# A gate's logits moved from two extra matmul columns to VectorE, in a fused attention and MLP kernel

## The chip, the cores and the metric

The kernel runs on one core of one Trainium2 chip. The metric is device microseconds of one execution; a kernel's time is the median of its runs. One execution is also profiled by the hardware, and its span, from the first to the last instruction of the program, is what the views of the profile show. The engines are TensorE (PE, its weight loads PEld), VectorE (DVE), ScalarE (ACT), GpSimd (POOL) and SyncE (SP), which here issues the DMAs.

## The reference

With S = 2048 tokens of D = 448 features, 16 heads of 28 and an MLP of F = 1792 features, all in float32:

```python
g = sigmoid((x * gate_w).sum(-1, keepdims=True))
a = A(x, wqkv, wo)          # q, k, v = x @ wqkv; each token attends to 8 keys, two tokens apart,
                            # itself the first; softmax; o = attn @ v; a = o @ wo
b = B(x, w1, b1, w2, b2)    # relu(x @ w1 + b1)**2 @ w2 + b2
return g * a + (1 - g) * b
```

The change concerns `(x * gate_w).sum(-1)`, one number for each token: the gate's logit.

## The kernel before

Every matrix product is made from two parts of each float32 number, a high part (the number rounded to the matmul's input type, made by ScalarE) and a low part (the rest, a subtraction by VectorE). A product is then three products: high x high, high x low, low x high. The tokens are cut into four chunks of 512, with features on the partitions: three slabs of 128 features and a last one of 64, which lies twice, in partitions 0 to 63 and 64 to 127. A chunk's raw features come by one load into a tile `raw` (two buffers, rotating, shared with the raw weights), and are split there.

Phase A makes q, k and v. A token tile is 128 tokens, and q, k or v of one tile is an accumulator in PSUM (`Acc`) of 448 columns; q's has 450, since the weight of the gate stands in two more columns behind q's (`ncols`, NQ = D + 2; two, one of them unused). ScalarE copies column 448 of q's accumulator into `zt` (L214) behind the copy of q itself (L206), one number for each token. The products run in pairs on the two halves of the array's rows (`side_by_side`, L187): a matmul of 64 rows for one accumulator on rows 0 to 63, and beside it one for another accumulator on rows 64 to 127. A "step" is one such pair. An accumulator has 21 matmuls of 64 rows: 9 on each half (three slabs, three products) and 3 with the last slab. When it has had all of one half it goes over to the other, and for that `turn` writes one element of its bank (a 1x1 memset by VectorE, L197; ScalarE, L195, in one place): the next matmul into the accumulator waits for that write, and the write waits for the last matmul before it. In chunk 0, q's slabs run on the full height (L258) as the data come, and q's last slab runs beside k's. In chunks 1 to 3, `qkv_two` does a block of two token tiles in 63 steps: 12 steps of q0 beside k1, 12 of q1 beside k0, 12 of v0 beside v1; and then, with the halves exchanged, 9 steps of each pair. The resets of (q0, k1), (q1, k0) and (v0, v1) are issued behind steps 24, 36 and 42 and needed at steps 36, 45 and 54. Chunk 0's v (42 steps) has them behind steps 15 and 24, needed at 24 and 33.

The order of the other work is set by a planner's clock: `advance` adds a price for each group of matmuls (203 ns for one pair of 448 columns), and issues what is due. `when(t, fn)` puts work at the clock time t, in ns; `at(dt, fn)` at dt from now. A chunk's splits are four pieces, 900 ns apart, at 19000 (chunk 1), 35000 (chunk 2) and 53500 (chunk 3); the next chunk's load is 4500 behind. So each engine has a fixed order of instructions, and an engine that waits holds up what stands behind it. Attention (GpSimd's multiplications, VectorE's sums) starts once chunks 0 and 1 are stored to DRAM, and goes on through phase B, where the MLP's products and those with `wo` run. There `gates` (L394 to L397) turns `zt` into the gate and one minus the gate.

SP issues all loads and stores, in the order of the program. q, k and v go to DRAM by L212, the raw x tiles come by L561, the splits of x go to DRAM by L140, and the MLP's biases come by L704 and L705. The pool `smp` has two buffers with the tag "lg", used in turn: `halo0` (zeros for the first tokens' keys), and then the attention's logits, a tile for each unit.

Of the kernel before, what the change touches and what calls it, by code (L numbers as in the profile page):

```python
# [7 lines left out]
F32 = mybir.dt.float32  # L8
F32R = mybir.dt.float32r
AF = mybir.ActivationFunctionType  # L10
ALU = mybir.AluOpType
AX = mybir.AxisListType

S, D, H, DH, W, F = 2048, 448, 16, 28, 8, 1792
P = 128
# [6 lines left out]
NF = F // P  # L22
CH = 512
NQ = D + 2
NP = 512


# [29 lines left out]
def gated_mix_kernel(ctx: ExitStack, tc: tile.TileContext, xT, wqkv, w1, w2, wo, b1, b2, out):  # L57
    nc = tc.nc

    def f32(ap):  # L60
        return ap.bitcast(F32)
# [4 lines left out]
    k_d = tc.dram_tile([2, G, SP + HALO, C], F32, name="k_d")  # L66
    v_d = tc.dram_tile([2, G, SP + HALO, C], F32, name="v_d")
    x_d = tc.dram_tile([3, 4, P, 2, CH], F32, name="x_d")
    f_d = tc.dram_tile([2, NS, P, D], F32, name="f_d")


# [20 lines left out]
    smp = ctx.enter_context(tc.tile_pool(name="smp", bufs=2))  # L92
# [4 lines left out]
    zt, gt, g1t = zg[:, 0:2], zg[:, 2:4], zg[:, 4:6]  # L97
# [14 lines left out]
    def split_full(raw, hi, lo, soon=now):  # L112
        nc.scalar.activation(hi, raw, AF.Copy)
        soon(lambda: nc.vector.tensor_sub(lo, raw, f32(hi)))

    def split_x78(raw, x7, x8, soon=now):

        split_full(raw, x7, x8, soon)
# [15 lines left out]
    def x_split(raw, x, k):  # L134

        split_full(raw[:, k], x.h[k], x.l[k])
# [14 lines left out]
    xcp = actx.enter_context(tc.tile_pool(name="phase_a_own", bufs=1, reuse_waits="tile"))  # L151
    wqh = ap.tile([P, 3, NP + 2 * D], F32R, name="wqh")
    wql = ap.tile([P, 3, NP + 2 * D], F32R, name="wql")

    w7h = ap.tile([P, NP + D], F32R, name="w7h")
    w7l = ap.tile([P, NP + D], F32R, name="w7l")
    ap.tile([P, 48], F32, name="pad_a")
# [3 lines left out]

    stage = {}

    def ncols(b):
        return NQ if b == 0 else D

    def block(b):

        o = (0, NP, NP + D)[b]
        return slice(o, o + ncols(b))  # L170

    class Acc:

# [26 lines left out]
    def qkv_evacuate(pt, c, tl, b):  # L200
        par, t = c // 2, (c % 2) * 4 + tl
        first = (b, t // 2) not in stage
        if first:
            stage[b, t // 2] = xap.tile([P, G, 2, C], F32, tag="stage", name=f"st{c}_{tl}_{b}", bufs=ST_BUFS)
        st = stage[b, t // 2]
        nc.scalar.activation(st[:, :, t % 2], pt[:, :D].rearrange("p (g c) -> p g c", g=G), AF.Copy)  # L206
        if not first:
            stage.pop((b, t // 2))
            t0 = t - t % 2
            dst, off = ((q_d, 0), (k_d, HALO), (v_d, HALO))[b]  # L210
            dd = dst[par, :, off:off + SP].rearrange("g (p s) c -> p g s c", s=NS)[:, :, t0:t0 + 2]
            nc.sync.dma_start(dd.rearrange("p g s c -> p g (s c)"), st.rearrange("p g s c -> p g (s c)"))  # L212
        if b == 0:
            nc.scalar.activation(zt[:, par, t:t + 1], pt[:, D:D + 1], AF.Copy)  # L214

    def full(x, acc, tl, b, ks=range(3)):
        sl, n = slice(tl * P, tl * P + P), block(b)
        r = []
        for k in ks:
            r += [(acc, x.h[k][:, sl], wqh[:, k, n]), (acc, x.h[k][:, sl], wql[:, k, n]),  # L220
                  (acc, x.l[k][:, sl], wqh[:, k, n])]
        return r

    def last(x, acc, tl, b):

        sl = slice(tl * P, tl * P + P)
        n = block(1) if b == 2 else slice(0, ncols(b))
        h, l = w7h[:, n], w7l[:, n]
        return [(acc, x.x7[:, sl], h), (acc, x.x7[:, sl], l), (acc, x.x8[:, sl], h)]

    def accs(c, b, tls, tags):
        return [Acc(t, f"qkv{c}_{tl}_{b}", ncols(b)) for t, tl in zip(tags, tls)]

    def run(c, todo, steps):

# [13 lines left out]
    def qkv_first(x):  # L249


        four = range(4)
        q = accs(0, 0, four, "bbbb")
        for k in range(3):
            for two in ((0, 1), (2, 3)):
                for j, prods in enumerate(zip(*(full(x, q[i], i, 0, (k,)) for i in two))):
                    for acc, a, w in prods:
                        nc.tensor.matmul(acc.pt[:, :NQ], a, w, start=k == j == 0, stop=False)  # L258
            advance(12 * MM448)
        for acc in q:  # L260
            acc.todo = 3
        k = accs(0, 1, four, "mmmm")
        t = [sum((last(x, a[i], i, b) for i in four), []) for b, a in ((0, q), (1, k))]
        f = [full(x, k[i], i, 1) for i in four]
        run(0, [t[0] + f[0] + f[1] + f[2] + f[3], t[1] + f[2] + f[3] + f[0] + f[1]],
            [(3, [(0, 0, q[0])], (k[0], k[0])),
             (12, [(0, i, q[i]) for i in (1, 2, 3)], (k[1], k[1])),
             (24, [], (k[0], k[2])), (33, [], (k[1], k[3])),
             (39, [(1, 0, k[0]), (1, 2, k[2])]), (48, [(1, 1, k[1]), (1, 3, k[3])])])
        v = accs(0, 2, four, "bbbb")  # L270
        f, l = [full(x, v[i], i, 2) for i in four], [last(x, v[i], i, 2) for i in four]
        run(0, [f[0] + l[0] + f[2] + l[2] + f[1] + f[3], f[1] + l[1] + f[3] + l[3] + f[0] + f[2]],
            [(15, [], (v[0], v[1])), (24, [], (v[2], v[3])),
             (33, [(2, 0, v[0]), (2, 1, v[1])]), (42, [(2, 2, v[2]), (2, 3, v[3])])])
# [196 lines left out]
    def soon(fn):  # L471
        at(LO_DELAY, fn)

    def advance(dt):
        clock["pe"] += dt
        while due := [x for x in later if x[0] <= clock["pe"]]:
            item = min(due, key=lambda x: x[0])
            later.remove(item)
            item[1]()
        if not clock["on"]:  # L480
            clock["att"] = clock["pe"]
            return
        while clock["att"] < clock["pe"]:
            try:
                r = next(att)
            except StopIteration:
                clock["on"] = False
                return
            if r is None:
                clock["att"] = clock["pe"]  # L490
                return
            clock["att"] += r


    def raw_tile(name):
        return rawp.tile([P, 4, 512], F32, tag="raw", name=name)
# [62 lines left out]
    def x_load(c):  # L559
        raw = raw_tile(f"xraw{c}")  # L560
        nc.sync.dma_start(raw[:, :, :CH], xT[c])  # L561
        return raw
# [68 lines left out]
    raws = [raw_tile("wqraw0")]  # L631
    rx = raw_tile("xraw0")
    for k in range(4):
        if k < 3:
            nc.sync.dma_start(raws[0][:, k, :NQ], wqkv[0, :, k])  # L635
        else:
            for b, rows in ((0, slice(0, 64)), (1, slice(64, P))):
                nc.sync.dma_start(raws[0][rows, k, :NQ], wqkv[b, rows, k])
        for cols in ((slice(0, 256), slice(256, CH)) if k == 0 else (slice(0, CH),)):
            nc.sync.dma_start(rx[:, k, cols], xT[0, :, k, cols])  # L640

    for b, tag in ((1, "k"), (2, "v")):
        raw = attp.tile([P, 3, D], F32, tag=tag, name=f"wqraw{b}")
# [4 lines left out]
    nc.sync.dma_start(raw7, wqkv[2, :, 3, :D])  # L648
    x = x_tiles(0, xap)
    for k in range(3):  # L650
        nc.scalar.activation(wqh[:, k, :NQ], raws[0][:, k, :NQ], AF.Copy)
        halves = (slice(0, 256), slice(256, CH))
        for i, cols in enumerate(halves):

            if k == i == 0:
                nc.vector.tensor_copy(x.h[k][:, cols], rx[:, k, cols])
            else:
                nc.scalar.activation(x.h[k][:, cols], rx[:, k, cols], AF.Copy)  # L658
        nc.vector.tensor_sub(wql[:, k, :NQ], raws[0][:, k, :NQ], f32(wqh[:, k, :NQ]))
        for cols in halves:  # L660
            nc.vector.tensor_sub(x.l[k][:, cols], rx[:, k, cols], f32(x.h[k][:, cols]))
    split_full(raws[0][:, 3, :NQ], w7h[:, :NQ], w7l[:, :NQ])
    split_x78(rx[:, 3], x.x7, x.x8)

    def wq_split(b, k):
        if k < 3:
            split_full(raws[b][:, k], wqh[:, k, block(b)], wql[:, k, block(b)])
        else:
            split_full(raw7, w7h[:, NP:], w7l[:, NP:])

    def when(t, fn, *args):
        later.append((t, lambda: fn(*args)))

    xs, xm = {0: x}, {}
    xraw = {1: x_load(1)}
# [30 lines left out]
        wq_split(1, k)  # L708
    for k in range(4):
        when(12000.0 + k * 900.0, wq_split, 2, k)  # L710
    for c, t in SPLIT_AT.items():
        when(t, x_begin, c)
        for k in range(4):
            when(t + k * 900.0, lambda c, k: x_split(xraw[c], xs[c], k), c, k)
        if c < 3:
            when(t + 4500.0, x_more, c + 1)
            when(t + 5000.0, lambda c: x_spill(c, xs[c]), c)
# [321 lines left out]
    c, x = ORDER[0], xm[3]  # L1039
# [8 lines left out]
    for g in range(2, 2 * NF):  # L1048
        i, f = g // (NF // 2), g % (NF // 2) * 2
        c = ORDER[i]  # L1050
# [118 lines left out]
```

## Time and profile before

| | us |
|---|---|
| median of 3 runs | 414.45 (414.34 to 414.81) |
| span of the profiled execution | 412.7 |
| TensorE busy in it | 408.2 |
| VectorE busy | 255.7 |
| ScalarE busy | 211.3 |
| GpSimd busy | 268.5 |

The page gives the profiled execution's span; of the time around it, it says nothing. A line of the timeline has: start in us from the span's start, duration in us, engine, line of the kernel, operation, names of out and in, shapes, and how many instructions of the same kind were merged, with the idle time before them and what ended it. A line of a group has, behind the bar, the busy time in us, the mean of one instruction in ns, and the idle time before. Matmuls are pipelined, so the duration of one (0.36 us) is longer than the distance from one to the next on the same rows; the distance is what counts. A line of windows has the stretch, its length, TensorE's busy time with the count of matmuls (a few records are missing), the granted clock, and the DMA's share and GB/s.

### The profile page before, as it was taken

The numbers are of one execution on the slowest core, as the hardware profiler recorded it, in microseconds if no ns is written. First come the engines' busy times: TensorE is split into PE (matmuls) and PEld (weight loads), VectorE is DVE, ScalarE is ACT, GpSimd is POOL, SyncE is SP. The second block draws the span as 40 slices with busy tenths as digits, with TensorE's granted clock in tenths as the row PEclk, the third lists the DMA queues.
The fourth block names the chain that finished last, engine by engine and source line by source line (L and its number), as shares of the span: only waits on it lengthen the run. The fifth ranks groups of instructions, "written<-read, shape, count | busy, mean of one in ns | idle before, by whom it ended". The sixth has DMA issues, their size and how long they took to land.

```text
span 412.7 us, 9327 instructions
## 1 busy us (share of the span) xinstructions
PE 408.2 (99%) x3835; PEld 378.0 (92%) x3835; DVE 255.7 (62%) x404; ACT 211.3 (51%) x477; POOL 268.5 (65%) x167
## 2 busy tenths in 40 slices
PE   8999999999999999999999999999999999999997
PEld 7999999999999999888888888989898888888996
DVE  4520433276767766777656798879576677891354
ACT  4641656388765565444565535444653254346540
POOL 0000001955999999989989899999899977940000
DMA  7989999969362315555112649764146630168304
GB/s 226 380 324 326 268 393 299 335 213 311 101 235 104 128 42 218 209 184 152 29 58 95 228 160 270 197 146 149 27 163 186 229 129 2 45 177 132 96 0 180
DMA packets 65611, 73.76 MB, mean 179 GB/s; under 512 B 32352, under 2 KB 58528, under 8 KB 65184
## 3 DMA queue, kind: packets, MB, share of 16 engines
q1 hardware_dynamic: 65568, 73.16, 55.1%
q8 instruction: 30, 0.49, 0.5%
q14 instruction: 13, 0.11, 0.1%
HBM read 45.71 MB, written 28.25 MB: 179 GB/s over the span
## 4 chain that ended last, share of the span: by engine, by line
PE 97%; DMA 1%; SPq 0%; DVE 0%; ACT 0%; issue 0%
PE b L187 33%; PE h L187 32%; PE qkv L187 23%; PE a L187 7%; PE qkv L258 1%; DMA xraw<-xT 1%; PE a L943 1%; PE last L943 0%; SPq L640 0%; SPq L635 0%; DVE bt L822 0%; ACT x L658 0%; PE last L935 0%; PE a L935 0%
## 5 line engine op out<-in xcount | busy, mean ns | idle before, releaser
L334 POOL TENSOR_TENSOR qk<-q,k 128x896 f32<-128x896 f32 x64 | 135.1, 2137 | 84.8 <-DMA k<-k_d 76.4
L341 POOL TENSOR_TENSOR av<-lg,v 128x896 f32<-128x896 f32 x64 | 119.4, 1961 | 6.3 <-DVE lg L335 5.8
L187 PE MATMUL qkv<-wqh,x 64*128 64x448 f32 (+1 forms) x528 | 89.1, 361 | 0.0
L615 DVE TENSOR_TENSOR h<-h,h 128x512 fp32r<-128x512 f32 x56 | 38.4, 688 | 65.9 <-ACT h L618 65.5
L187 PEld LDWEIGHTS qkv<-wqh,x 64*128 64x128 f32 x528 | 72.2, 184 | 0.8
L187 PE MATMUL qkv<-wql,x 64*128 64x448 f32 (+1 forms) x264 | 72.2, 360 | 0.0
L187 PE MATMUL b<-w2ah,h 64*128 64x448 f32 x448 | 68.5, 359 | 0.0
L187 PE MATMUL b<-w2bh,h 64*128 64x448 f32 x448 | 67.8, 360 | 0.0
L335 DVE TENSOR_REDUCE lg<-qk 128x32 f32<-128x896 f32 x64 | 67.0, 1074 | 0.0
L349 DVE TENSOR_REDUCE o<-av 128x112 f32<-128x896 f32 x64 | 66.4, 1070 | 0.1
L616 ACT ACTIVATE h<-h,b1z 128x512 f32<-128x512 f32 x56 | 36.7, 655 | 43.6 <-PE h L187 43.6
L187 PEld LDWEIGHTS b<-w2ah,h 64*128 64x128 f32 x448 | 46.9, 184 | 2.8
L187 PEld LDWEIGHTS b<-w2bh,h 64*128 64x128 f32 x448 | 45.3, 184 | 3.2 <-ACT h L567 0.3
L187 PEld LDWEIGHTS qkv<-wql,x 64*128 64x128 f32 x264 | 44.5, 184 | 0.4
L187 PE MATMUL b<-w2al,h 64*128 64x448 f32 x224 | 44.3, 358 | 0.0
L187 PE MATMUL b<-w2bl,h 64*128 64x448 f32 x224 | 43.2, 358 | 0.0
L206 ACT ACTIVATE st<-qkv 128x448 f32<-128x448 f32 x48 | 24.3, 546 | 34.8 <-PE qkv L187 26.9
L617 ACT ACTIVATE h<-h 128x512 fp32r<-128x512 f32 x56 | 33.5, 598 | 1.7
L618 ACT ACTIVATE h<-h 128x512 f32<-128x512 f32 x56 | 33.3, 594 | 0.0
L187 PE MATMUL h<-x,w1h 64*128 64x512 f32 x168 | 32.8, 386 | 0.0
L567 ACT ACTIVATE h<-h 128x4 fp32r<-128x4 f32 (+1 forms) x35 | 7.2, 207 | 43.1 <-PE b L187 43.0
L187 PE MATMUL h<-x2b,w1h 64*128 64x512 f32 x168 | 28.2, 386 | 0.0
(145 smaller groups left out, 728.7 us busy)
## 6 DMA issues: line engine op xcount, KB each, us to landing
k<-k_d SPq DMA_DIRECT2D x8, 840.0 KB, 6.4
v<-v_d SPq DMA_DIRECT2D x8, 840.0 KB, 4.8
x_d<-x SPq DMA_DIRECT2D x11, 512.0 KB, 6.6
q_d<-st SPq DMA_DIRECT2D x8, 448.0 KB, 4.1
k_d<-st SPq DMA_DIRECT2D x8, 448.0 KB, 4.6
v_d<-st SPq DMA_DIRECT2D x8, 448.0 KB, 5.9
w1raw<-w SPq DMA_DIRECT2D x4, 896.0 KB, 9.2
q<-q_d SPq DMA_DIRECT2D x8, 448.0 KB, 3.6
```

The source lines that it names most:

```text
L187: nc.tensor.matmul(acc.pt[:, :acc.n], a[rows], w[rows], start=acc.todo == acc.all, stop=acc.todo == 1)
L206: nc.scalar.activation(st[:, :, t % 2], pt[:, :D].rearrange("p (g c) -> p g c", g=G), AF.Copy)
L258: nc.tensor.matmul(acc.pt[:, :NQ], a, w, start=k == j == 0, stop=False)
L334: nc.gpsimd.tensor_mul(pr, q[:, s:s + 1].to_broadcast([P, W, C]), k[:, s:s + W])
L335: pending.append(lambda: nc.vector.tensor_reduce(lg[:, s], pr.rearrange("p w (h d) -> p w h d", h=HG), axis=AX.X, op=ALU.add))
L341: nc.gpsimd.tensor_mul(pr.rearrange("p (h d) w -> p w h d", h=HG), lg[:, s][:, :, :, None].to_broadcast([P, W, HG, DH]), v[:, s:s + W].rea ...
L349: nc.vector.tensor_reduce(o[:, g * C:(g + 1) * C], pr, axis=AX.X, op=ALU.add)
L567: nc.scalar.activation(ap, f32(ap), AF.Copy)
L615: nc.vector.tensor_sub(hl, pt, f32(hh))
L616: ops += [lambda pt=pt, r=r: nc.scalar.activation(pt, pt, AF.Relu, bias=b1t[:, f + r:f + r + 1]), lambda pt=pt, hh=hh: nc.scalar.activatio ...
L617: lambda pt=pt, hh=hh: nc.scalar.activation(hh, pt, AF.Square),
L618: lambda pt=pt, r=r, low=low: (nc.scalar.activation(pt, pt, AF.Square), at(delays[r], low))]
```

## The change

q's accumulators get 448 columns; `ncols` goes, and so does the copy of column 448 (L214). The logits are made by VectorE from the raw features: for each chunk, `z_product` multiplies slab 0 by its weight (one number for each partition, `gw`) and adds slabs 1, 2 and the last (64 partitions) by fused multiply-adds into a tile `zu` of 128x512. `z_sums` transposes `zu` in blocks of 32x32 and sums each block's 32 numbers: for each token four partial sums remain, in four blocks of partitions. After the last chunk these are stored to DRAM (32 KB) and loaded back by four loads so that the four partial sums of a token stand in one partition, and `z_last` adds them into `zt`. The tile `zs` that holds them takes the second "lg" buffer, so the attention's tiles exchange buffers. The products stand between the splits of the same chunk, 450 ns behind each by the planner's clock.

```diff
-    def ncols(b):
-        return NQ if b == 0 else D
...
-        return slice(o, o + ncols(b))
+        return slice(o, o + D)
...
-        if b == 0:
-            nc.scalar.activation(zt[:, par, t:t + 1], pt[:, D:D + 1], AF.Copy)
...
-        return [Acc(t, f"qkv{c}_{tl}_{b}", ncols(b)) for t, tl in zip(tags, tls)]
+        return [Acc(t, f"qkv{c}_{tl}_{b}", D) for t, tl in zip(tags, tls)]
...
-                        nc.tensor.matmul(acc.pt[:, :NQ], a, w, start=k == j == 0, stop=False)
+                        nc.tensor.matmul(acc.pt[:, :D], a, w, start=k == j == 0, stop=False)
...
+    zs = smp.tile([P, 3, NZ], F32, tag="lg", name="zs")
+    zu = xcp.tile([P, CH], F32, tag="zu", name="zu")
+    zpart, zall, gw = zs[:, 0], zs[:, 1], zs[:, 2, 0:4]
+    nc.vector.tensor_copy(gw, raws[0][:, :, D])
+    def z_product(raw, k):
+        r = slice(0, P if k < 3 else 64)
+        if k:
+            nc.vector.scalar_tensor_tensor(zu[r], raw[r, k], gw[r, k:k + 1], zu[r], op0=ALU.mult, op1=ALU.add)
+        else:
+            nc.vector.tensor_scalar_mul(zu, raw[:, 0], gw[:, 0:1])
+    def z_sums(c):
+        nc.vector.transpose(zu, zu)
+        nc.vector.tensor_reduce(
+            zpart.rearrange("p (b c t) -> p c t b", b=4, c=4)[:, c],
+            zu.rearrange("p (t b r) -> p t b r", t=4, b=4), axis=AX.X, op=ALU.add)
+    def z_store():
+        nc.sync.dma_start(z_d, zpart)
+    def z_load():
+        for b in range(4):
+            nc.sync.dma_start(
+                zall[b * 32:b * 32 + 32].rearrange("p (a n) -> p a n", a=4),
+                z_d[:, b * 16:b * 16 + 16].rearrange("(a c) n -> c a n", a=4))
+    def z_last():
+        nc.vector.tensor_reduce(
+            zt.rearrange("p q s -> p (q s)"), zall.rearrange("p (a n) -> p n a", a=4), axis=AX.X, op=ALU.add)
...
+    for k in range(4):
+        when(15000.0 + k * 700.0, z_product, rx, k)
+    when(17900.0, z_sums, 0)
+    when(60500.0, z_store)
+    when(76000.0, z_load)
+    when(86500.0, z_last)
     for c, t in SPLIT_AT.items():
         when(t, x_begin, c)
         for k in range(4):
             when(t + k * 900.0, lambda c, k: x_split(xraw[c], xs[c], k), c, k)
+            when(t + k * 900.0 + 450.0, lambda c, k: z_product(xraw[c], k), c, k)
+        when(t + 4200.0, z_sums, c)
```

More of the change, by code (lines that the diff above doesn't have):

```diff
@@ L24 @@
 NQ = D + 2
+NZ = 64
 NP = 512
@@ L68, in gated_mix_kernel @@
     x_d = tc.dram_tile([3, 4, P, 2, CH], F32, name="x_d")
+    z_d = tc.dram_tile([P, NZ], F32, name="z_d")
     f_d = tc.dram_tile([2, NS, P, D], F32, name="f_d")
@@ L226, in last @@
         sl = slice(tl * P, tl * P + P)
-        n = block(1) if b == 2 else slice(0, ncols(b))
+        n = block(1) if b == 2 else slice(0, D)
         h, l = w7h[:, n], w7l[:, n]
@@ L650, in gated_mix_kernel @@
     for k in range(3):
-        nc.scalar.activation(wqh[:, k, :NQ], raws[0][:, k, :NQ], AF.Copy)
+        nc.scalar.activation(wqh[:, k, :D], raws[0][:, k, :D], AF.Copy)
         halves = (slice(0, 256), slice(256, CH))
@@ L658, in gated_mix_kernel @@
                 nc.scalar.activation(x.h[k][:, cols], rx[:, k, cols], AF.Copy)
-        nc.vector.tensor_sub(wql[:, k, :NQ], raws[0][:, k, :NQ], f32(wqh[:, k, :NQ]))
+        nc.vector.tensor_sub(wql[:, k, :D], raws[0][:, k, :D], f32(wqh[:, k, :D]))
         for cols in halves:
             nc.vector.tensor_sub(x.l[k][:, cols], rx[:, k, cols], f32(x.h[k][:, cols]))
-    split_full(raws[0][:, 3, :NQ], w7h[:, :NQ], w7l[:, :NQ])
+    split_full(raws[0][:, 3, :D], w7h[:, :D], w7l[:, :D])
     split_x78(rx[:, 3], x.x7, x.x8)
+    zs = smp.tile([P, 3, NZ], F32, tag="lg", name="zs")
[23 more added lines that the diff above has]
+            zt.rearrange("p q s -> p (q s)"), zall.rearrange("p (a n) -> p n a", a=4), axis=AX.X, op=ALU.add)
     def wq_split(b, k):
```

## The prediction

> **What bounds the kernel now.** I read the page first: engines' shares, then the waits of TensorE.
>
> ```profile
> span 412.7 us, 9327 instructions
> PE 408.2 (99%) x3835; PEld 378.0 (92%) x3835; DVE 255.7 (62%) x404; ACT 211.3 (51%) x477; POOL 268.5 (65%) x167
> PE 97%; DMA 1%; SPq 0%; DVE 0%; ACT 0%; issue 0%
> ```
>
> TensorE is busy for 99% of the span and makes 97% of the chain that ended last. Its list of waits has two entries, both before 9 us:
>
> ```profile
> PE warm L628 <- DVE b1z L626: 1.2, 1, 1.2
> PE qkv L258 <- ACT x L658: 0.3, 1, 0.3
> ```
>
> So time can be won only by fewer or faster matmuls, and lost only where some other engine makes TensorE wait where it does not now. The change takes two columns from q's products, 450 to 448. What a column costs is read from the timeline of TensorE, in a place where one row half runs q (450) and the other k (448):
>
> ```profile
> 35.03 0.36 PE L187 MATMUL qkv<-w7h,x 64*128 64x448 f32 x1
> 35.23 0.36 PE L187 MATMUL qkv<-w7l,x 64*128 64x448 f32 x1
> 35.24 0.55 PE L187 MATMUL qkv<-w7h,x 64*128 64x450 f32 x2
> 35.44 0.37 PE L187 MATMUL qkv<-w7l,x 64*128 64x450 f32 x1
> 35.65 0.37 PE L187 MATMUL qkv<-w7h,x 64*128 64x450 f32 x1
> 35.86 0.53 PE L187 MATMUL qkv<-wqh,x 64*128 64x448 f32 x2
> ```
>
> 448 columns step by 0.200 us (35.03 to 35.23). 450 columns step by 0.207 us (35.24, 35.44, 35.65, 35.86: 0.62 us in three steps). Two columns cost 6.7 ns, far more than 2/448 of 200 ns (0.9 ns). The same shows in whole blocks. These windows are cut at the first 450-column product of each block of 63 steps (two token tiles: q, k and v); the first window is chunk 0's v, 42 steps of 448 columns alone:
>
> ```profile
> 22.50:30.90 8.40, 8.40 (x87) 1.00 0.88 309
> 30.90:43.66 12.76, 12.76 (x130) 1.00 0.94 313
> 43.66:56.42 12.76, 12.76 (x129) 1.00 1.00 320
> 56.42:69.18 12.76, 12.76 (x129) 1.00 1.00 323
> 69.18:81.94 12.76, 12.76 (x128) 1.00 0.99 341
> 81.94:94.72 12.78, 12.78 (x127) 1.00 0.73 243
> ```
>
> 8.40/42 is 0.200 us a step. A block of 63 such steps would take 12.60 us and takes 12.76. The missing 0.16 us is exactly 24 steps of 6.7 ns: in a block's first part q0 and then q1 run 12 steps each on the same row half (9 full, 3 of the last 64 features). In the second part q has 9+9 steps on the other half, 0.12 us, which the lead of that half covers. The granted clock (1.00) is full throughout.
>
> **The change part by part.**
>
> Removed, q's two columns. Six blocks at 0.16 us are 0.96 us (the sixth, from 94.72, has MLP work beside it but the same 24 steps). In chunk 0, the 12 last-feature products of q run beside k's: 12 x 6.7 ns = 0.08 us. Chunk 0's 36 full-height products are 450 wide too, but step by 0.200 already:
>
> ```profile
> 9.82 0.96 PE L258 MATMUL qkv<-wqh,x 128*128 128x450 f32 x4
> ```
>
> (busy 0.96 us for four: three steps of 0.200 and the 0.36 us of the last), so I take 0 there; bounds 0 and 36 x 6.7 ns = 0.24. Sum: 1.04 us. The Trainium skill, "TensorE: Matmul & The Clock Gate", section Back-to-back issue gap, gives an isolated warm gap of N/2.4 + 2.5 ns, so an estimate of 0.8 ns for two columns; by it the sum would be 156 x 0.8 ns = 0.13 us and no measurable change. The trace disagrees (200 and 207 ns where the page gives 189 and 190), and the measurement decides.
>
> Removed, 16 copies of the logit column on ScalarE.
>
> ```profile
> L214 ACT ACTIVATE zg<-qkv x16: 142/166/191, 14.2 to 109.5; 128x1 f32<-128x1 f32 x16
> ```
>
> 16 x 0.17 us on an engine that is 51% busy and for which TensorE never waits: nothing.
>
> Added, VectorE work: for each of four chunks a scaling (128x512), three fused multiply-adds, a transposition and a sum over 32. Prices, by the nearest groups:
>
> ```profile
> L822 DVE SCALAR_TENSOR_TENSOR bt<-b,zg,bt 128x448 f32<-128x448 f32 x16 | 10.2, 680 | 7.9 <-PE b L187 7.8
> L114 DVE TENSOR_TENSOR x<-xraw,x 128x512 fp32r<-128x512 f32 x13 | 8.4, 690 | 14.1 <-ACT x L113 14.1
> L661 DVE TENSOR_TENSOR x<-xraw,x 128x256 fp32r<-128x256 f32 x6 | 2.4, 422 | 1.8 <-ACT x L658 1.8
> L656 DVE CAST x<-xraw 128x256 fp32r<-128x256 f32 x1 | 0.3, 294 | 2.6 <-DMA xraw<-xT 2.6
> L352 DVE STREAM_TRANSPOSE o<-o 128x448 f32<-128x448 f32 x16 | 10.2, 638 | 0.3
> L349 DVE TENSOR_REDUCE o<-av 128x112 f32<-128x896 f32 x64 | 66.4, 1070 | 0.1
> ```
>
> An element costs (690-422)/256 = 1.05 ns. Multiply-add at 512: 680+67 = 0.75 us, about 0.68 from start to start where the next does not depend on it. Scaling: one source, like the cast, 256 elements in 294 ns; at 512 between 0.43 (fixed part 155 ns, half the slope) and 0.69; I take 0.43, nearest the cast. Transposition 0.71, sum 1070-384x1.05 = 0.67. A chunk costs 4.1 us, all four 16 us on an engine 62% busy. What matters is what queues behind them: the resets of a PSUM accumulator (1x1 memsets, L197) that let its second row half go on. Chunk 1's splits, from the timeline of VectorE, and TensorE's step 24 of v:
>
> ```profile
> 19.21 0.62 DVE L114 TENSOR_TENSOR w7l<-wqraw,w7h 128x448 fp32r<-128x448 f32 x1
> 24.23 1.93 DVE L114 TENSOR_TENSOR x<-xraw,x 128x512 fp32r<-128x512 f32 x3 [4.40 <-ACT x L113]
> 25.52 0.06 DVE L197 MEMSET qkv<- 1x1 f32 x2
> 27.52 0.09 DVE L197 MEMSET qkv<- 1x1 f32 x2 [0.75 <-PE qkv L187]
> 27.23 0.43 PE L187 MATMUL qkv<-wqh,x 64*128 64x448 f32 x2
> ```
>
> Chunk 0's sums fit the gap from 19.83 to 24.23 (4.1 of 4.4 us). Then in the new order: split 0.62, scaling 0.37, split 0.62, first resets (25.9, needed at 27.23), multiply-add, split, multiply-add, split (2.6): second resets done by 28.6. They are needed at step 33, 27.23 + 9 x 0.2 = 29.03. Some 0.35 us is left after the handover. For chunk 2 and chunk 3:
>
> ```profile
> 41.90 1.29 DVE L114 TENSOR_TENSOR x<-xraw,x 128x512 fp32r<-128x512 f32 x2 [3.19 <-ACT x L113]
> 46.81 0.06 DVE L197 MEMSET qkv<- 1x1 f32 x2
> 58.34 2.54 DVE L114 TENSOR_TENSOR x<-xraw,x 128x512 fp32r<-128x512 f32 x4 [5.84 <-ACT x L113]
> 61.60 0.14 DVE L197 MEMSET qkv<- 1x1 f32 x2 [0.72 <-PE qkv L187]
> ```
>
> Chunk 2: splits, products, sums (6.4 us from 41.90) and two w1 splits (1.2): reset at 49.5, needed at 43.66 + 36 x 0.2 = 50.86; 1.1 us left. Chunk 3: before the second reset stand 4 splits and 6 new instructions, 6.5 us from 58.34: 64.9, needed at 56.42 + 45 x 0.2 = 65.42; about 0.45 left. So I price the stalls at 0. Bounds: 0 from below (a longer VectorE queue shortens nothing), above with the scaling at 0.69 and the sum 0.4 dearer, 0.3 us in all.
>
> Moved, the buffers. The raw x tiles are held by the products too: the load of chunk 1 (issued at 11.31) also waits for the copy of the weight column, about 0.7 us later; chunk 3's (46.17) for chunk 2's last product, some 0.9 later.
>
> ```profile
> 11.31 0.33 SPq L561 DMA_DIRECT2D xraw<-xT  x1
> 46.17 0.50 SPq L561 DMA_DIRECT2D xraw<-xT  x1
> DMA to landing us min/median/max: 2.5/5.6/7.9
> ```
>
> With the longest landing of such a load, 7.9 us, they are there by 19.9 and 55.0; the splits that use them reach VectorE at 24.23 and 58.34. The two "lg" buffers trade places, which orders nothing new in time. Nothing.
>
> Added, DMAs on SP: one store of 32 KB and four loads of 64-byte runs, due at clock 60.5 and 76.0 of the planner, that is near 65 and 82 us. Ahead of v's store:
>
> ```profile
> 74.44 1.11 SPq L704 DMA_DIRECT2D b1z<-b  x1
> 83.20 0.67 SPq L212 DMA_DIRECT2D v_d<-st  x1
> ```
>
> b1's load has runs of 56 bytes and takes 1.11 us to issue; four such are 4.4 at most, so v_d of chunk 2 goes up to 3 us later. Only unit 4 of the attention reads it, much later. The last sum (0.2 us) comes behind the third reset of chunk 3's first block, near 92. The four loads are issued by 86 and land by 92 (median above) to 94 (longest). What VectorE would lose there it has idle before the next resets, near 100:
>
> ```profile
> 98.30 0.63 DVE L518 TENSOR_TENSOR w2al<-copy,w2ah 128x448 fp32r<-128x448 f32 x1 [1.71 <-ACT copy L513]
> ```
>
> I price it at 0, with a bound of 0.3 us (2 us late less 1.7 idle).
>
> Sum: -1.04 us on the profiled span, 412.7 to 411.7. The page gives no time of that execution outside its span; the median of the runs is 414.45, 1.75 more, and I let that stand: 413.4.
>
> **The rivals.**
> 1. The columns are not the cause of 0.207 (two unequal streams, or uneven issue, and the step stays). Every 12.76 against 12.60, with 24 steps to account for it, speaks against; that 450 columns at full height step by 0.200 speaks for. The Trainium skill's gap rule, named above, would lead here too. Time 414.3 to 414.45. Half the effect, or 0.3 to 0.5 us lost in resets (second bound above), ends in the same class: about 413.9.
> 2. The resets come late and TensorE stalls: slower. Let each added VectorE instruction cost e more than my price. The stalls are 3e-0.35 (chunk 1), 6e-1.1 (chunk 2), 6e-0.45 (chunk 3), together 15e-1.9. The gain is gone at e = 0.20 us, at 0.25 it is slower by 0.2%, at 0.30 the time is 414.45-1.04+2.6 = 416.0. The prices rest on measured groups of the same operations, which speaks against; that multiply-adds with both operands in SBUF appear in no row speaks for.
>
> **How the numbers follow.** 0.2% (0.83 us) is about what a measurement of this kernel can tell from no change. My sum of 1.04 is only a little above it. Main case, gain of 0.85 to 1.2: 0.55. Rival 1 with the partial cases: 0.30. Rival 2: 0.15. So faster 0.55, same 0.30, slower 0.15. The main case's own range is 413.1 to 413.6 (with 0.24 more at the full-height products, or 0.2 lost). For 8 in 10 it reaches through rival 1 and the beginning of rival 2: 413.0 to 414.9.
>
> **What would show it.** After: blocks of 12.60 us and steps of 0.200 in q; the same two waits of TensorE and none on L197; multiply-adds of 0.75 us; the second resets of chunk 1 near 0.4 us before step 33; span 411.7. The prediction is wrong if blocks stay at 12.76, if TensorE waits for a memset near 29, 51 or 65 us, or if a later engine gives the 1 us back.

## The result

The median went from 414.56 us (22 runs, 414.33 to 416.12) to 413.81 us (22 runs, 413.37 to 415.26). The ratio is 0.9978, with a 95% interval of 0.997 to 0.9987: 0.9 us by the ratio (0.5 to 1.2 by the interval), 0.75 by the medians, where 1.04 had been forecast. On another chip the same two kernels gave 0.9969 (0.9956 to 0.9983).

The page of the changed kernel (busy time, share of the span and instructions of each engine):

```profile
span 412.0 us, 9325 instructions
PE 407.2 (99%) x3835; PEld 371.7 (90%) x3835; DVE 270.5 (66%) x430; ACT 210.5 (51%) x461; POOL 268.5 (65%) x167
```

Its TensorE's waits: us in total, their count, and the longest in us:

```profile
PE warm L625 <- DVE b1z L623: 1.2, 1, 1.2
PE qkv L255 <- ACT x L655: 0.3, 1, 0.3
```

VectorE's share rose from 62% to 66%, by 15 us of work, and TensorE waits for the same two things as before. The gain is in the pace of phase A. These rows of TensorE's timeline are the first step with the last slab (the tenth step) of the six blocks of 63 steps:

```profile
32.58 0.36 PE L186 MATMUL qkv<-w7h,x 64*128 64x448 f32 x2
45.18 0.36 PE L186 MATMUL qkv<-w7h,x 64*128 64x448 f32 x2
57.78 0.36 PE L186 MATMUL qkv<-w7h,x 64*128 64x448 f32 x2
70.38 0.36 PE L186 MATMUL qkv<-w7h,x 64*128 64x448 f32 x2
82.98 0.37 PE L186 MATMUL qkv<-w7h,x 64*128 64x448 f32 x2
95.65 0.39 PE L186 MATMUL qkv<-w7h,x 64*128 64x448 f32 x2
```

The first five are 12.60 us apart, where the kernel before takes 12.76; the last distance is 12.67, where it takes 12.78. VectorE's new work, by groups (busy time, mean ns; the last slab's four multiply-adds, on 64 partitions, are a group of their own), and chunk 1's splits in its timeline:

```profile
L671 DVE SCALAR_TENSOR_TENSOR zu<-xraw,zs,zu 128x512 f32<-128x512 f32 x8 | 6.0, 746 | 0.1
L677 DVE STREAM_TRANSPOSE zu<-zu 128x512 f32<-128x512 f32 x4 | 2.8, 711 | 0.1
L678 DVE TENSOR_REDUCE zs<-zu 128x16 f32<-128x512 f32 x4 | 2.8, 688 | 0.1
L673 DVE TENSOR_SCALAR zu<-xraw,zs 128x512 f32<-128x512 f32 x4 | 1.9, 480 | 0.0
```

```profile
24.11 0.69 DVE L116 TENSOR_TENSOR x<-xraw,x 128x512 fp32r<-128x512 f32 x1 [0.18 <-ACT x L115]
24.72 0.48 DVE L673 TENSOR_SCALAR zu<-xraw,zs 128x512 f32<-128x512 f32 x1
25.80 0.06 DVE L196 MEMSET qkv<- 1x1 f32 x2
28.36 0.06 DVE L196 MEMSET qkv<- 1x1 f32 x2
```

Chunk 0's sums were done 0.18 us before chunk 1's first split, and the second resets were done at 28.4, some 0.5 us before step 33 needed them.

To see where the time came from, two places are compared that every version passes: the first step with the last slab in chunk 0, and ScalarE's first activation of the MLP, at the end of phase A. First the kernel before, then the changed one:

```profile
12.71 0.47 PE L187 MATMUL qkv<-w7h,x 64*128 64x450 f32 x2
111.25 0.66 ACT L616 ACTIVATE h<-h,b1z 128x512 f32<-128x512 f32 x1 [0.87 <-PE h L187]
```

```profile
12.67 0.48 PE L186 MATMUL qkv<-w7h,x 64*128 64x448 f32 x2
110.37 0.66 ACT L613 ACTIVATE h<-h,b1z 128x512 f32<-128x512 f32 x1 [0.94 <-PE h L186]
```

From the one place to the other the kernel before takes 98.54 us and the changed one 97.70: 0.84 us less. The start up to 12.7 us depends on when the first loads land (ScalarE's first splits wait for them), and among the profiled executions below it lies between 12.39 and 13.02 wherever nothing was changed in it. That is why single spans differ by a few tenths. Phase B changed little: VectorE's last instruction comes at 409.72 before and at 408.79 after, 0.93 earlier, and the span is 0.75 shorter (412.73 and 411.98), since from there to the end it took 3.01 us before and 3.19 after. The last store lies in that stretch.

### The profile page after: what moved, and what is told of

Its sections match the earlier page's. It is cut to its first block, busy times and chain, and to the rows that moved or that the text cites. A ratio compares the mean times of both kernels' runs of the same rounds, so it can differ in the third digit from the quotient of the medians.

```text
span 412.0 us, 9325 instructions
## 1 busy us (share of the span) xinstructions
PE 407.2 (99%) x3835; PEld 371.7 (90%) x3835; DVE 270.5 (66%) x430; ACT 210.5 (51%) x461; POOL 268.5 (65%) x167
## 4 chain that ended last, share of the span: by engine, by line
PE 97%; DMA 1%; SPq 0%; DVE 0%; ACT 0%; issue 0%
PE b L186 33%; PE h L186 32%; PE qkv L186 23%; PE a L186 7%; PE qkv L255 1%; DMA xraw<-xT 1%; PE a L984 1%; PE last L984 0%; SPq L637 0%; SPq L632 0%; DVE bt L863 0%; ACT x L655 0%; PE last L976 0%; PE a L976 0%
## 5 line engine op out<-in xcount | busy, mean ns | idle before, releaser
L186 PE MATMUL qkv<-wqh,x 64*128 64x448 f32 x528 | 78.6, 359 | 0.0
L186 PEld LDWEIGHTS qkv<-wqh,x 64*128 64x128 f32 x528 | 50.7, 184 | 2.7
L186 PE MATMUL qkv<-wql,x 64*128 64x448 f32 x264 | 48.8, 359 | 0.0
L186 PEld LDWEIGHTS b<-w2bh,h 64*128 64x128 f32 x448 | 42.8, 184 | 3.3 <-ACT h L564 0.3
L186 PEld LDWEIGHTS b<-w2ah,h 64*128 64x128 f32 x448 | 43.1, 184 | 2.9
L186 PE MATMUL b<-w2al,h 64*128 64x448 f32 x224 | 41.2, 358 | 0.0
L186 PE MATMUL b<-w2bl,h 64*128 64x448 f32 x224 | 41.1, 358 | 0.0
L186 PE MATMUL h<-x,w1h 64*128 64x512 f32 x168 | 29.6, 386 | 0.0
L186 PE MATMUL h<-x0b,w1h 64*128 64x512 f32 x168 | 28.1, 386 | 0.0
L186 PE MATMUL h<-x1b,w1h 64*128 64x512 f32 x168 | 28.1, 386 | 0.0
```

Source lines behind the costliest of these rows:

```text
L186: nc.tensor.matmul(acc.pt[:, :acc.n], a[rows], w[rows], start=acc.todo == acc.all, stop=acc.todo == 1)
```

## The experiments

**The removal alone.** The logits are left out: zeros stand in their place.

```diff
-    zs = smp.tile([P, 3, NZ], F32, tag="lg", name="zs")
...
-        when(t + 4200.0, z_sums, c)
+    nc.gpsimd.memset(zt, 0.0)
```

> The removal alone: q's accumulators have 448 columns and the gate's logits are left out (zeros instead, no work on VectorE, no DMAs for them). Theory: the whole gain comes from the two columns and VectorE's work is hidden, so the time is that of the changed kernel, 413.5 to 413.8 us, span 411.6 to 412.0, and TensorE at the end of phase A is 0.88 us ahead of the kernel before (within 0.05). Rival: VectorE's work or its DMAs took back the missing 0.15 us of my 1.04; then this one is 1.0 us or more ahead at that place and at 413.3 or below.

Measured: 413.64 us (9 runs), ratio 0.9978 (0.9969 to 0.9988), span 411.6.

```profile
12.39 0.48 PE L186 MATMUL qkv<-w7h,x 64*128 64x448 f32 x2
110.09 0.66 ACT L613 ACTIVATE h<-h,b1z 128x512 f32<-128x512 f32 x1 [0.93 <-PE h L186]
```

At the second place it is 1.16 us ahead of the kernel before, more than my theory allowed. But 0.32 of that is there at the first place, and between the two it takes 97.70 us, the same as the changed kernel. The expectation had not reckoned with the start; the stretch that the change touches is equal to 0.01 us. So VectorE's sums, the store and the four loads cost nothing there.

**The addition alone.** VectorE makes the logits, and q keeps 450 columns.

```diff
+    def ncols(b):
+        return NQ if b == 0 else D
...
-        return slice(o, o + D)
+        return slice(o, o + ncols(b))
...
```

> The addition alone: logits by VectorE as in the changed kernel, but q's products keep their 450 columns (the copy of column 448 is left out, since nobody reads it). Theory: blocks of 63 steps stay at 12.76 us and the time is that of the kernel before within 0.15 us (414.4 to 414.6). Rival 1 (the gain comes from elsewhere, such as ScalarE's 16 copies): this one gains 0.5 us or more. Rival 2 (VectorE's work costs): it is slower than before by 0.2 us or more.

Measured: 414.65 us (11 runs), ratio 1.0004 (0.9995 to 1.0013), span 412.8.

```profile
12.74 0.47 PE L189 MATMUL qkv<-w7h,x 64*128 64x450 f32 x2
111.27 0.66 ACT L616 ACTIVATE h<-h,b1z 128x512 f32<-128x512 f32 x1 [0.93 <-PE h L189]
```

The stretch takes 98.53 us, as before (98.54). 16 copies on ScalarE are gone here too, so neither they nor VectorE's work move anything. The two halves of the change add up: all of the 0.84 us is in the two columns.

**How near VectorE's work is to costing something.** The changed kernel, with one more multiply-add (by zero) behind each product.

```diff
             nc.vector.scalar_tensor_tensor(zu[r], raw[r, k], gw[r, k:k + 1], zu[r], op0=ALU.mult, op1=ALU.add)
+            nc.vector.scalar_tensor_tensor(zu[r], raw[r, k], 0.0, zu[r], op0=ALU.mult, op1=ALU.add)
...
+            nc.vector.scalar_tensor_tensor(zu, raw[:, 0], 0.0, zu, op0=ALU.mult, op1=ALU.add)
```

> The changed kernel with each product of the logits followed by one more multiply-add by zero, so the logits stay the same and VectorE's work for them nearly doubles (16 more instructions of about 0.75 us). It tests the room that I worked out in front of the accumulator resets. Theory (the resets are the place where late VectorE work turns into TensorE time, with about 0.4 to 0.6 us of room in chunk 1, 1.1 in chunk 2, 0.45 in chunk 3): chunk 0's chain runs 2.8 us over its gap and pushes chunk 1's resets some 4 us late, chunk 2's go 1.5, chunk 3's 2.4; TensorE waits for memsets near 29, 51 and 65 us, 6 to 9 us in all, time 420 to 423. Rival (the resets are far from limiting): TensorE waits for nothing and the time stays at 413.8.

Measured: 421.98 us (2 runs), ratio 1.018 (1.0162 to 1.0199). TensorE's first wait (us in total, count, the longest):

```profile
PE qkv L186 <- DVE qkv L196: 7.0, 5, 1.9
```

Where in its timeline these waits fall (in brackets, the idle time and who ended it):

```profile
29.08 0.48 PE L186 MATMUL qkv<-wqh,x 64*128 64x448 f32 x2 [1.95 <-DVE qkv L196]
33.07 0.47 PE L186 MATMUL qkv<-wqh,x 64*128 64x448 f32 x2 [1.91 <-DVE qkv L196]
56.20 0.47 PE L186 MATMUL qkv<-wqh,x 64*128 64x448 f32 x2 [1.25 <-DVE qkv L196]
69.57 0.47 PE L186 MATMUL qkv<-wqh,x 64*128 64x448 f32 x2 [0.48 <-DVE qkv L196]
73.07 0.47 PE L186 MATMUL qkv<-wqh,x 64*128 64x448 f32 x2 [1.41 <-DVE qkv L196]
```

The waits are for the accumulator resets (L196), 3.9 us in chunk 1's splits, 1.3 in chunk 2's and 1.9 in chunk 3's, where some 4, 1.5 and 2.4 were expected. So the mechanism of the slower rival is real, and its point lay where the room of the prediction had put it: 12 us more on an engine busy for two thirds of the span cost 8 us, of which 7.0 are these waits, because they stand in front of the resets.

**What a column costs: equal streams.** The kernel before with 450 columns in k's and v's products as well.

```diff
     def ncols(b):
-        return NQ if b == 0 else D
+        return NQ
...
```

> The kernel before with 450 columns in k's and v's products too, so that both row halves run equal streams. Theory (the cost of a matmul goes in lots of 16 columns, 64 bytes of a row; 450 pays for 464): each step of a pair costs 0.2067 us on both halves, a block 13.02 us instead of 12.76, chunk 0's v 8.68 instead of 8.40, the time about 2 us more than before (416 to 417). Rival (450 beside 448 is slow because the two streams are unequal): equal streams step by 0.2008 or less, a block takes 12.65 or less and the time falls below 414.0.

Measured: 415.65 us (5 runs), ratio 1.0032 (1.002 to 1.0045). Its timeline, at the tenth step of two blocks in a row:

```profile
45.73 0.36 PE L187 MATMUL qkv<-w7h,x 64*128 64x450 f32 x2
58.64 0.36 PE L187 MATMUL qkv<-w7h,x 64*128 64x450 f32 x2
```

A block takes 12.91 us, 204.9 ns a step. That is less than the 206.7 of my theory and far more than the 200.8 of the rival. Unequal streams are not the cause; at most 2 of the 6.7 ns go with them. Two reservations: 204.9 is a mean (single steps of this kernel lie between 199 and 218 ns, most of them at 202 to 204), and its weight tiles are wider, so that v's weights lie at another place than before.

**What a column costs: wider q.** Three more widths, with columns of zeros.

```diff
-        return NQ if b == 0 else D
+        return NW if b == 0 else D          # NW = 464, then 456 and 480
...
```

> The kernel before with q's products 464 columns wide (14 columns of zeros behind the 450). Theory of lots of 16 columns: 464 costs what 450 does, blocks of 12.76 us, time within 0.2 us of before. Rival (proportional: each further column adds 0.42 ns to the 6.7 that two columns cost): 24 steps of 212.5 ns, blocks of 12.90 us, time 415.2 to 415.4.

> The kernel before with q 456 columns wide (6 of them zeros), to see how the price of columns beyond 448 grows: 450 cost 6.7 ns a step and 464 cost 10.2, by the blocks of 63 steps (24 such steps make the difference to 12.60 us). One theory (a fixed 6 ns as soon as a step leaves 448, and 0.26 ns for each column): 8.2 ns, blocks of 12.80 us. Other theory (each column 1/2.4 ns, and a misfit that depends on the width's rest in lots of 64, nothing at 448 and 512): between 6 and 10 ns without order; blocks 12.74 to 12.84 don't tell them apart, a block of 12.76 or less speaks against the first. The start may be some 2.6 us later, since the zeros are written first; the blocks count, not the time.

> The same with q 480 columns wide. A fixed 6 ns and 0.26 ns a column: 14.4 ns, blocks of 12.94 us. Each column 1/2.4 ns and no misfit at 480: 13.3 ns, blocks of 12.92. With a misfit of 3 ns or more as at 464: 16.5 ns, blocks of 13.0 us.

Measured: 417.94 us for 464 (4 runs; ratio 1.0072, 1.0052 to 1.0092), 415.99 for 456 (8 runs; 1.0032, 1.0019 to 1.0045), 419.21 for 480 (2 runs; 1.0108, 1.0079 to 1.0137). 2 to 3 us of each are in the start, which waits for the zeros. The blocks tell the price; a window of each, cut at the first wide product, with its length, TensorE's busy time and its products. First 456 columns:

```profile
45.91:58.69 12.78, 12.78 (x130) 1.00 0.99 316
```

Then 464:

```profile
46.44:59.30 12.86, 12.86 (x129) 1.00 0.98 317
```

And 480:

```profile
46.77:59.80 13.03, 13.03 (x129) 1.00 0.99 321
```

Against 12.60 us and over 24 steps, a step costs 6.7 ns more at 450 columns, 7.5 at 456, some 10.6 at 464 and 18 at 480. The theory of lots of 16 columns falls: 464 does not cost what 450 does. The proportional rival falls too (12.90 at 464), and so does a fixed 6 ns with 0.26 ns a column (12.94 at 480). What fits these four widths, made after the fact, is about 0.42 ns for each column and some 4 to 6 ns on top. The MLP's 512 columns do not pay this: they step by 226.7 ns in both kernels, 64 columns of 0.42 ns above 448. What the extra 4 to 6 ns are stays open, and 450 columns do not always pay them. In the second part of the block from 30.90, q's 18 steps of 450 columns took 200.3 ns each in the kernel before; these two rows of its timeline are nine steps apart:

```profile
39.24 0.38 PE L187 MATMUL qkv<-wqh,x 64*128 64x450 f32 x2
41.04 0.38 PE L187 MATMUL qkv<-wqh,x 64*128 64x450 f32 x2
```

The same holds for the second parts of the third, fourth and sixth block (200 to 201 ns); in those of the second and the fifth a step took some 206. The price belongs to the width together with something else that these runs do not name.

**Why chunk 3 gained less: the place of a slab.** In the changed kernel chunk 3 still has slow steps, with 448 columns. The first of three last-slab steps and the first step behind them, in chunk 3 and then in chunk 2:

```profile
82.98 0.37 PE L186 MATMUL qkv<-w7h,x 64*128 64x448 f32 x2
83.60 0.36 PE L186 MATMUL qkv<-wqh,x 64*128 64x448 f32 x2
```

```profile
57.78 0.36 PE L186 MATMUL qkv<-w7h,x 64*128 64x448 f32 x2
58.38 0.36 PE L186 MATMUL qkv<-wqh,x 64*128 64x448 f32 x2
```

Three steps take 0.62 us in chunk 3 and 0.60 in chunk 2. Chunk 3's last slab alone lies in the pool that the MLP reads (`xpool`). Two kernels move slabs.

```diff
-        xs[c] = X(own + xm[c].t[3:])
+        xs[c] = X(own[:2] + xm[c].t[2:3] + own[2:])
...
```

> The changed kernel, in which chunk 3's steps with the last slab still take 0.207 us with 448 columns (9 of 63 in each half). In chunk 3 that slab alone lies in another pool (the one that the MLP reads). Here the places are exchanged: the third slab lies there and the last slab in phase A's own tiles; everything else is the same. Place theory: the slow steps move to the third slab (18 in each half), blocks of chunk 3 take 12.72 us instead of 12.66, time 0.1 us more. Slab theory: the last slab's steps stay at 0.207, blocks 12.66. If neither, blocks of 12.60 and the time 0.1 us below the changed kernel's.

Measured: 414.0 us (11 runs), ratio 0.9986 (0.9977 to 0.9994), beside 413.73 for the changed kernel in the same session. The stretch between the two places is 0.13 us longer (97.83), as expected; the rest of the 0.3 us is not accounted for, since the two profiled executions start alike (first place at 13.02 and 12.98). The first of the third slab's steps, of the last slab's (83.35), and the first step behind them:

```profile
82.73 0.37 PE L186 MATMUL qkv<-wqh,x 64*128 64x448 f32 x2
83.35 0.37 PE L186 MATMUL qkv<-w7h,x 64*128 64x448 f32 x2
83.95 0.37 PE L186 MATMUL qkv<-wqh,x 64*128 64x448 f32 x2
```

The slow steps have moved to the third slab (0.62 us for three), and the last slab's take 0.60.

The other kernel puts chunk 2's last slab into that pool, and makes the copy that would overwrite it later.

```diff
-            xs[c] = x_tiles(c, xap)
+            xs[c] = X([xap.tile([P, 2, CH], F32R, tag=f"x{j}", name=f"x{c}_{j}") for j in range(3)] +
+                      [xpool.tile([P, 2, CH], F32R, tag="x0", name=f"x{c}_3")])
...
```

> The changed kernel, with chunk 2's last slab in the pool that holds chunk 3's (the slow place), everything else as it was but the time of one copy. Chunk 2 runs from 56 to 81 us, and GpSimd begins its attention work at 72. If the place alone makes a step slow: chunk 2's last-slab steps take 0.207 us from the start, both blocks 12.66 us. If it is the traffic of the attention beside the place: they take 0.200 before 72 and 0.207 behind it, blocks of 12.60 and 12.66. If the place has no part in it: 0.200 throughout.

Chunk 2's first last-slab step, and the first step behind the three:

```profile
57.66 0.37 PE L186 MATMUL qkv<-w7h,x 64*128 64x448 f32 x2
58.28 0.36 PE L186 MATMUL qkv<-wqh,x 64*128 64x448 f32 x2
```

The three take 0.62 us, at 58 us, with GpSimd's attention work beginning at 70.5. So it is the place and not the attention's traffic. The time was 414.15 us (8 runs), ratio 0.9989 (0.9978 to 1.0), with the stretch 0.13 us longer than the changed kernel's. Whether a place outside that pool for chunk 3's last slab would win some 0.1 us was not tried; no run here is faster than the changed kernel and computes the logits.

## Why the prediction was right, and where its sum was off

The forecast (faster by a little more than 0.2%, 413.4 us) came out with the right sign and the right mechanism, 0.4 us too low by the median of 22 runs. 0.1 of this is the kernel before, whose median over 22 runs is 414.56 in place of 414.45; the rest is a gain that came out smaller than the sum. 413.81 lies inside the wide range (413.0 to 414.9) and outside the main case's own (413.1 to 413.6), which was too narrow.

- **A step's price, 6.7 ns for two columns, and 0.16 us a block.** Right for the four blocks of chunks 1 and 2, which gained 0.16 each. The reading from the block lengths held. The estimate by the gap rule of the Trainium skill ("TensorE: Matmul & The Clock Gate", section Back-to-back issue gap), 0.13 us in all, did not; the measurement decides. The sentence on a block's second part (9+9 steps, 0.12 us, covered by the lead of that half) is right for two blocks of six only: in the other four these steps cost next to nothing, as shown above. The sum did not suffer, since it took nothing for them, but 6.7 ns is not a price that 450 columns pay everywhere.
- **"Six blocks at 0.16 us are 0.96 us."** This is the term that was mis-sized. Of 0.32 us for the last two blocks, 0.11 and 0.01 came. The window 81.94:94.72 had 12.78 us, and I took its block as one more of the same kind, and the sixth without a window. In the fifth, 6 of the 24 steps are last-slab steps, slow before and after; the other 18 at 6.7 ns are 0.12 us, close to the 0.11 measured. A look at the sixth block in the trace before would have told it; these rows are steps of q1 with 450 columns, beside k0, six steps apart:

```profile
97.19 0.36 PE L187 MATMUL qkv<-wqh,x 64*128 64x450 f32 x1
98.39 0.36 PE L187 MATMUL qkv<-wqh,x 64*128 64x450 f32 x1
```

  Six steps in 1.20 us: q1's nine steps paid nothing for their columns here, so there was nothing to win with them. And the last slab's steps in chunk 3 are slow for the place they lie in, with 448 columns as with 450. The two experiments on the place show the latter; why the former is free in that block was only seen, not tried. q0's nine steps ahead of them did pay, some 5 ns each (94.72 to 96.57), and why none of these 0.05 us shows in the block's gain stays open.
- **Chunk 0, 0.08 us.** Measured 0.07 in the lagging half, between the first and the last of these steps. Full-height products at 0: in agreement. Eighteen of these steps in a row take 3.60 us in both kernels (8.82 to 12.42 before, 8.77 to 12.37 after).
- **VectorE's work at 0.** Right. The multiply-add at 0.75 us was 0.746, the transposition at 0.71 was 0.711, the sum at 0.67 was 0.688, the scaling at 0.43 was 0.480, nearest to the cast as taken. The room of some 0.35 us in chunk 1 was about 0.5. The kernel with twice the products shows the stalls where the rival had put them.
- **Buffers and DMAs at nothing.** Right. The loads of the partial sums took 4.0 us to issue, where up to 4.4 had been allowed for. From the timeline of SP's queue:

```profile
47.34 0.46 SPq L558 DMA_DIRECT2D xraw<-xT  x1
81.14 4.04 SPq L689 DMA_DIRECT2D zs<-z_d  x4
```

  Chunk 3's load was issued 1.2 us later than before in this execution (47.34 for 46.17, 0.9 forecast), and 0.6 later (46.79) in another one of the same kernel. GpSimd's first work on the attention began at 72.12 in this execution and at 71.19 in the kernel before. That is no cost of the change: in the other execution of the changed kernel it began at 70.84, and in the kernel without VectorE's products at 71.84. In this execution it was ahead again by its next wait, for VectorE, at 85.
- **Phase B gives nothing back.** Right: 0.88 us ahead at its beginning, 0.93 at the end.

## What to carry to other kernels

Where the bound engine runs in equal steps, measure a whole block of them and divide by the count: a width that looks 0.4% larger cost 3% of a step in most places and nothing in some. Do that for each block that is to be in the sum, also for those that look like more of the same; two of six were not. Work on an engine with idle time is free only as far as what queues behind it has room, and that room can be counted in the trace before: half a microsecond here, found to within 0.2.

## What was not expected of the hardware

- With two matmuls side by side on the two halves of the rows, a step takes 200.0 ns at 448 columns and 226.7 at 512, but some 207.5 at 456 and 210.6 at 464, and in most places 206.7 at 450: 4 to 6 ns more than the columns account for. At 450 there are blocks in which the same steps take 200 to 201 ns. At full height 450 columns step by 200 ns in the kernel before, no more than 448 do in the changed one; in the kernel in which k and v are 450 wide too, the full-height steps from 8.8 to 12.2 us take 198 to 210 ns, 203 in the mean.
- The same stationary slab costs 200.0 ns a step from one pool and 206.7 from another, with all else equal and no other engine at work on attention. Three tiles of that pool were slow as the stationary side. What it is about these places was not tried.
